# Weight tiles read in runs of two rows (4 KB), two modes on the two halves of the partitions, with the spectrum and the mode products laid out to match

## The chip, the cores and the metric

The kernel runs on one core of one Trainium2 chip. The metric is the device time of one execution in microseconds (us). The kernel before takes 456.14 us, the median of three runs (455.82 to 456.61). The profile is of one execution and spans 453.8 us.

The engines are named as in the profile: PE is TensorE (matmuls; PEld its loads of the stationary operand), DVE is VectorE, ACT is ScalarE, POOL is GpSimd (here it mostly issues transfers), SP is SyncE. SBUF is the memory on the core with 128 partitions, PSUM the memory that the matmuls write.

## The reference

The work has two parts: an attention over 8 batches, 8 heads, 576 positions and 64 values per head, and on its output a spectral mixing with 64 modes, and a residual layer.

```python
# attention, per batch and head
scores = q @ k.T / 8
bias   = -(cum[:, None] - cum[None, :])        # cum = cumsum(max(s, 0))
attn   = softmax(where(causal, -1e9, scores + minimum(bias, 0)))
x      = attn @ v                              # heads side by side: x is [8, 576, 512]

# spectral mixing: w_r, w_i are [64 modes, 512, 512] in float32
X  = rfft(x, axis=1)[:, :64]                   # Xr, Xi
Yr = einsum('bmd,mde->bme', Xr, w_r) - einsum('bmd,mde->bme', Xi, w_i)
Yi = einsum('bmd,mde->bme', Xr, w_i) + einsum('bmd,mde->bme', Xi, w_r)
u  = x + irfft(Yr + 1j * Yi, n=576)
out = u + maximum(u @ w_ch, 0)
```

The two weight tensors hold 2 x 64 x 512 x 512 float32 values, 134.2 MB. Each is used for only eight rows (the batches), so they pass through the core once.

## The kernel before

The 512 channels are taken in NG = 4 groups of 128 (`g`), a group being two heads. There are N = 32 steps of attention (`n`), one for each channel group and batch. The spectrum of a step's output is taken one step later (`fft`), and as soon as a channel group has all its batches, its 64 modes are multiplied with the weights, in NCK = 8 mode groups of MC = 8 modes (`modes(g, c)`). The weights stream in all the while.

A weight tile holds four modes of one channel group: 128 partitions (channels `d`) x 4 modes x 512 (`e`), bf16, 512 KB written and 1 MB of float32 read. There are 128 such tiles, four for each `(g, c)`: real and imaginary (`ri`), even and odd modes (`par`). They go to rings of 11 and 6 buffers, the first eight to places that are free early. GpSimd issues the loads of q, k, v and the weights in one order.

```python
def loads_w(upto):
    ...
        src = (moe_w_r, moe_w_i)[ri]
        todo.append((
            t,                                             # [128, 4, 512] bf16
            src[c * MC + par : (c + 1) * MC : 2, g * P : (g + 1) * P, :].rearrange("m p e -> p m e"),
        ))
        wt[key] = t
    return todo

def load(*lists):                                          # interleaves lists of loads
    todo = [((i + 0.5) / len(l), x) for l in lists for i, x in enumerate(l)]
    for _, (dst, src) in sorted(todo, key=lambda t: t[0]):
        nc.gpsimd.dma_start(out=dst, in_=src)
```

In memory a row of 512 float32 values (2 KB) is contiguous, and the rows of one mode follow each other; a partition takes one row of each of four modes.

The spectrum of one step is a matmul of the step's output (stationary, 128 positions x 128 channels) with a table of sines and cosines (moving, 3 x 64 columns), over five tiles of positions. The result, 128 channels x 192, is cast to bf16 into `xs`, in an order that lets one slice of 32 columns hold 16 values of the spectrum (two of real and imaginary, eight batches) and 16 zeros.

```python
xs = [gp.tile([P, 5, 2, B, NM], BF16, name=f"xs{i}") for i in range(2)]

def fft(n):
    ...
    ps = auxpool.tile([P, 3 * NM], FP32, name="ft_ps", tag="aux")
    for T in range(NT):                                    # NT = 5
        nT = tails[T]
        nc.tensor.matmul(ps, x_all[:nT, g, b, T, :], Ff_sb[:nT, T, :],
                         start=(T == 0), stop=(T == NT - 1))
    for ri in range(2):
        nc.vector.tensor_copy(
            out=xs[g % 2][:, 3 - 2 * ri, :, b, :],
            in_=ps[:, (1 - ri) * NM : (3 - ri) * NM].rearrange("p (r m) -> p r m", r=2),
        )
```

The mode products of one `(g, c)` are 16 matmuls: for each of the four weight tiles (`x`) four modes, each in its own column group (`cg`, 32 output rows) of the array. The zeros in the stationary operand let an even and an odd mode share the 32 output rows of a column group: the even mode adds to 16 of them, the odd mode to the other 16.

```python
def modes(g, c, meanwhile=None):
    ps = auxpool.tile([P, DM], FP32, name="yp", tag="aux")
    for x in range(4):
        ri, par = divmod(x, 2)
        cols = xs[g % 2].rearrange("p k r b m -> p (k r b) m")
        c0 = (48, 16)[ri] - 16 * par
        if meanwhile and x in meanwhile:
            meanwhile[x]()
        for cg in range(4):
            nc.tensor.matmul(
                ps[32 * cg : 32 * cg + 32, :],
                cols[:, c0 : c0 + 32, c * MC + 2 * cg + par],
                wt[(g, c, ri, par)][:, cg, :],
                start=(x == 0), stop=(x == 3),
                tile_position=(0, 32 * cg), skip_group_check=True,
            )
    ...                                                    # sum over g in y_acc (VectorE)
```

After the last step only the mode groups of the last channel group remain (c = 0 to 7), mixed with other products, and then the end: inverse transform, the product with `w_ch`, and the stores. `meanwhile` is used for the very last mode group alone (c = 7): work that needs no weights is put between its tiles.

Of the kernel before, what the change touches and what calls it, by code (L numbers as in the profile page):

```python
# [9 lines left out]
FP32 = mybir.dt.float32  # L10
FP16 = mybir.dt.float16
BF16 = mybir.dt.bfloat16
# [6 lines left out]
def kernel(  # L19
# [26 lines left out]
    MC = 8  # L46
# [7 lines left out]
    W = 2 * P  # L54
    NWN = S // W
    NK = 2 * NWN


    ident_np = np.eye(P, dtype=np.float32)
# [7 lines left out]
    m_idx = np.arange(NM, dtype=np.float64)  # L67
    ang = 2.0 * np.pi * np.outer(t_idx, m_idx) / S
    Ff_np = np.zeros((SP, 3 * NM), dtype=np.float16)
    Ff_np[:S, :NM] = np.sin(ang)  # L70
    Ff_np[:S, NM : 2 * NM] = np.cos(ang)
    Ff_np[:S, 2 * NM :] = -np.sin(ang)
    cmv = np.where(m_idx == 0, 1.0, 2.0) / S
    G_np = np.zeros((NM, 2, SP), dtype=np.float64)
    G_np[:, 0, :S] = cmv[:, None] * np.cos(ang.T)
# [16 lines left out]
    gp = ctx.enter_context(tc.tile_pool(name="globals", bufs=1))  # L92


    x_all = gp.tile([P, NG, B, NT, P], FP16, name="x_all")
    y_acc = gp.tile([P, NCK, DM], FP32, name="y_acc")

    xs = [gp.tile([P, 5, 2, B, NM], BF16, name=f"xs{i}") for i in range(2)]
    ident16h = gp.tile([P, P], FP16, name="ident16h")
    Ff_sb = gp.tile([P, NT, 3 * NM], FP16, name="Ff_sb")  # L100
    G_sb = gp.tile([P, SP], FP16, name="G_sb")
# [4 lines left out]
    auxpool = ctx.enter_context(tc.tile_pool(name="aux_psum", bufs=2, space=PSUM))  # L106
# [24 lines left out]
    p_sb = [ap_.tile([P, poff[-1]], FP16, name=f"p_sb{i}") for i in range(NP_)]  # L131
    p4 = [ap_.tile([P, P], FP16, name=f"p4_{i}") for i in range(2)]

    temp = xs[1].rearrange("p k r b m -> p (k r b m)").bitcast(FP32)
    ident32, negm32, s_sb = temp[:, :P], temp[:, P : P + 2 * W + NL], temp[:NPAIR, -S:]
    ident16 = ap_.tile([P, P], BF16, name="ident16")
    negm = ap_.tile([P, 2 * W + NL], BF16, name="negm")
# [49 lines left out]
    wt = {}  # L187
# [8 lines left out]
    def loads_w(upto):  # L196
        todo = []
        while len(wt) < min(upto, len(wq)):
            g, c, ri, par = key = wq[len(wt)]
            i = ring_of(len(wt))  # L200
            if i is None:
                t = early[len(wt)]
            else:
                t = (wpool, wpool2)[i].tile([P, WM, DM], BF16, name="w_sb", tag="w")
            src = (moe_w_r, moe_w_i)[ri]
            todo.append((
                t,
                src[c * MC + par : (c + 1) * MC : 2, g * P : (g + 1) * P, :].rearrange("m p e -> p m e"),
            ))
            wt[key] = t  # L210
        return todo

# [15 lines left out]
    for n in range(N):  # L228
# [3 lines left out]
        while nt < min(w, len(wq)):  # L232
            i = ring_of(nt)
# [37 lines left out]
    with tc.tile_pool(name="cum_psum", bufs=1, space=PSUM) as cpsum:  # L271
# [5 lines left out]
            out=cum, data0=spos, data1=zer, initial=0.0, op0=ALU.add, op1=ALU.add  # L277
# [133 lines left out]
    def fft(n):  # L411
        if n < 0:
            return
        g, b = divmod(n, B)
        ps = auxpool.tile([P, 3 * NM], FP32, name="ft_ps", tag="aux")
        for T in range(NT):
            nT = tails[T]
            nc.tensor.matmul(  # L418
                ps,
                x_all[:nT, g, b, T, :],  # L420
                Ff_sb[:nT, T, :],
                start=(T == 0), stop=(T == NT - 1),
            )
        for ri in range(2):
            nc.vector.tensor_copy(
                out=xs[g % 2][:, 3 - 2 * ri, :, b, :],
                in_=ps[:, (1 - ri) * NM : (3 - ri) * NM].rearrange("p (r m) -> p r m", r=2),
            )

    def modes(g, c, meanwhile=None):  # L430


        ps = auxpool.tile([P, DM], FP32, name="yp", tag="aux")
        for x in range(4):
            ri, par = divmod(x, 2)
            cols = xs[g % 2].rearrange("p k r b m -> p (k r b) m")
            c0 = (48, 16)[ri] - 16 * par
            if meanwhile and x in meanwhile:
                meanwhile[x]()
            for cg in range(4):  # L440
                nc.tensor.matmul(  # L441
                    ps[32 * cg : 32 * cg + 32, :],
                    cols[:, c0 : c0 + 32, c * MC + 2 * cg + par],
                    wt[(g, c, ri, par)][:, cg, :],
                    start=(x == 0), stop=(x == 3),
                    tile_position=(0, 32 * cg), skip_group_check=True,
                )
        if g == 0:
            nc.vector.tensor_copy(out=y_acc[:, c, :], in_=ps)
        elif g < NG - 1:  # L450
            nc.vector.tensor_tensor(out=y_acc[:, c, :], in0=ps, in1=y_acc[:, c, :], op=ALU.add)
        else:
            yb = spool.tile([P, DM], FP16, name="y_sb", tag="y")
            for cols in halves if c == NCK - 1 else [slice(0, DM)]:
                nc.vector.tensor_tensor(
                    out=yb[:, cols], in0=ps[:, cols], in1=y_acc[:, c, cols], op=ALU.add
                )
            if c >= NCK - 2:
                spread(c, 0, yb)
            return yb  # L460
# [59 lines left out]
    with tc.tile_pool(name="sc_psum", bufs=2, space=PSUM) as scpool, \  # L520
            tc.tile_pool(name="tr_psum", bufs=1, space=PSUM) as trpool, \
            tc.tile_pool(name="av_psum", bufs=1, space=PSUM) as avpool:
        cum_rows(0)
        transposes(0, 0)
        transposes(0, 1)
        load(loads_qkv(2))
        pad_p()
        for n in range(N):
            if n in (0, 2):
                nc.vector.memset(xs[n // 2].rearrange("p k r b m -> p (k r b m)").bitcast(FP32), 0.0)  # L530
            tails_due = loads_tails(n // B + 1)[n % B - 3 : n % B - 2] if 2 < n % B < 5 else []
            load(loads_qkv(n + LA) + tails_due, loads_w(on_chip[n]))
            cum_rows(n + 1)
            scores(n, 0)
            av(n - 1, 1)
            transposes(n + 1, 0)
            scores(n, 1)
            i = first_pairs[n - N + len(first_pairs)] if n >= N - len(first_pairs) else None
            if i is not None:
                first_transposed(i, 0)  # L540
            transposes(n + 1, 1)
            fft(n - 1)
            av(n, 0)
            if i is not None:
                first_product(i, 0)
                first_transposed(i, 1)
            for c in mode_steps.get(n, []):
                modes(c // NCK, c % NCK)
            if i is not None:
                first_product(i, 1)  # L550
            if n == N // 2:
                nc.gpsimd.dma_start(out=wch_sb, in_=moe_w_ch.rearrange("(dt p) e -> p dt e", p=P))
        av(N - 1, 1)
        fft(N - 1)
# [10 lines left out]
    zpool = ctx.enter_context(tc.tile_pool(name="z_psum", bufs=2, space=PSUM))  # L565

    NLOC = 4
    old = xs[0].rearrange("p k r b m -> p (k r b m)")
    xt_sb = [
        old[:, i * 2 * DM : (i + 1) * 2 * DM].bitcast(FP16).rearrange("p (x t c) -> p x t c", x=2, c=P)  # L570
        for i in range(2)
# [199 lines left out]
    c = NCK - 2  # L771
# [112 lines left out]
```

The softmax here doesn't subtract the row's maximum and nothing guards it: scores larger than these inputs give would overflow.

## Time and profile before

| | before |
|---|---|
| time, median of 3 | 456.14 us |
| span of the profile | 453.8 us |
| PE busy | 340.4 us (75%), 4233 instructions |
| DVE busy | 241.0 us (53%), 535 instructions |
| ACT busy | 221.9 us (49%), 390 instructions |
| POOL busy | 183.0 us (40%), 269 instructions |
| weight loads by POOL, 512 KB written each | 120 to the rings and 8 to early places; median 11.9 us from issue to landing in the rings |
| spectrum: matmuls 128*128, 192 columns | 160, median 253 ns each (five overlap to 0.69 us) |
| spectrum: casts to `xs`, 128 x 128 | 64, mean 277 ns |
| mode products 128*32, 512 columns | 512, median 379 ns each (four column groups overlap) |

Busy time counts only the instructions of an engine. The DMA row of the profile is of the 16 engines that move data; its GB/s are the bytes written, so that a load that turns float32 into bf16 shows half of what it reads. The chain of waits follows the work that ended last back in time, at each step to what released it: what is on it sets the end, what is not is hidden.

### The profile page before, as it was taken

The numbers are of one execution on the slowest core, as the hardware profiler recorded it, in microseconds if no ns is written. First come the engines' busy times: TensorE is split into PE (matmuls) and PEld (weight loads), VectorE is DVE, ScalarE is ACT, GpSimd is POOL, SyncE is SP. The second block draws the span as 40 slices with busy tenths as digits, with TensorE's granted clock in tenths as the row PEclk, the third lists the DMA queues.
The fourth block names the chain that finished last, engine by engine and source line by source line (L and its number), as shares of the span: only waits on it lengthen the run. The fifth ranks groups of instructions, "written<-read, shape, count | busy, mean of one in ns | idle before, by whom it ended". The sixth has DMA issues, their size and how long they took to land.

```text
span 453.8 us, 10370 instructions
## 1 busy us (share of the span) xinstructions
PE 340.4 (75%) x4233; PEld 218.6 (48%) x4265; DVE 241.0 (53%) x535; ACT 221.9 (49%) x390; POOL 183.0 (40%) x269
## 2 busy tenths in 40 slices
PE   1779887976563979836677857688889678879995
PEld 1456665654342656624445535456554335534332
DVE  7775665753242656723436434446655443562796
ACT  1585877464242656724435444455551323431774
POOL 6655554554344565434364444444433231200000
PEclk9996999998576889968878899889996986999999
DMA  9999999999999999999999999999999999995688
GB/s 176 200 203 203 202 201 204 202 204 204 205 204 202 201 203 202 205 205 204 202 196 203 204 204 203 204 203 202 206 207 208 207 206 206 207 214 109 232 298 317
DMA packets 108511, 93.75 MB, mean 207 GB/s; under 512 B 28384, under 2 KB 103648, under 8 KB 108464
## 3 DMA queue, kind: packets, MB, share of 16 engines
q0 software_dynamic: 98960, 81.81, 113.8%
q1 hardware_dynamic: 9504, 11.29, 7.8%
q8 instruction: 33, 0.54, 0.4%
q14 instruction: 14, 0.11, 0.1%
HBM read 164.56 MB, written 9.44 MB: 383 GB/s over the span
## 4 chain that ended last, share of the span: by engine, by line
DMA 51%; PE 31%; DVE 8%; issue 4%; POOL 2%; ACT 2%; SPq 0%; DVEq 0%; POOLq 0%; ACTq 0%
DMA w_sb<-in_moe_w_i_dram 21%; DMA q<-in_q_dram 15%; DMA w_sb<-in_moe_w_r_dram 11%; PE sc_ps L365 4%; PE av_ps L394 4%; PE z_ps L602 3%; PE yp L441 3%; PE sc_ps L359 3%; PE tr_ps L324 3%; DMA k<-in_k_dram 2%; PE z_ps L693 2%; PE g_ps L652 2%; PE ft_ps L418 2%; PE u_ps L712 2%; PE u_ps L693 1%
## 5 line engine op out<-in xcount | busy, mean ns | idle before, releaser
L373 ACT ACTIVATE p_sb<-sc_ps,cumt_sb 128x576 f16<-128x576 f32 (+1 forms) x256 | 141.7, 635 | 45.6 <-PE sc_ps L365 45.0
L217 POOL DMA_DIRECT2D w_sb<-in_moe_w_i_dram x60 | 45.1, 751 | 85.0 <-PE yp L441 37.6
L217 POOL DMA_DIRECT2D w_sb<-in_moe_w_r_dram x60 | 45.3, 757 | 63.5 <-DMA w_sb<-in_moe_w_r_dram 28.2
L217 POOL DMA_DIRECT2D v<-in_v_dram x72 | 50.8, 708 | 32.0 <-DMA w_sb<-in_moe_w_r_dram 7.4
L324 PE MATMUL tr_ps<-ident,q 64*64 64x64 bf16 x576 | 17.5, 210 | 54.3 <-DMA q<-in_q_dram 54.3
L359 PE MATMUL sc_ps<-negm,ident 128*128 128x256 bf16 x256 | 55.5, 303 | 0.2
L327 DVE COPY qtA<-tr_ps 64x576 bf16<-64x576 bf16 x32 | 23.8, 743 | 49.6 <-PE tr_ps L324 49.5
L441 PE MATMUL yp<-w_sb,xs 128*32 128x512 bf16 x480 | 36.5, 406 | 14.1 <-DMA w_sb<-in_moe_w_i_dram 11.1
L344 ACT ACTIVATE p<-sc_ps,cumt 128x64 f16<-128x64 f32 x32 | 10.0, 313 | 74.3 <-PE sc_ps L340 74.3
L394 PE MATMUL av_ps<-v,p_sb 128*128 128x65 f16 x1024 | 44.5, 198 | 0.0
L394 PEld LDWEIGHTS <-p_sb 128*128 128x128 f16 x1024 | 39.5, 100 | 4.9 <-issue 0.8
L327 DVE COPY ktA<-tr_ps 64x576 bf16<-64x576 bf16 x32 | 24.0, 749 | 33.6 <-PE tr_ps L324 33.6
L324 PEld LDWEIGHTS <-q 64*64 64x64 bf16 x576 | 13.7, 123 | 57.0 <-DMA q<-in_q_dram 56.3
L365 PE MATMUL sc_ps<-qtB,ktB 128*128 128x64 bf16 (+2 forms) x160 | 34.9, 324 | 3.5 <-issue 2.4
L365 PE MATMUL sc_ps<-qtA,ktA 65*128 65x512 bf16 (+2 forms) x192 | 36.5, 299 | 0.7 <-DMA qtA<-ncum_sb 0.7
L399 DVE TENSOR_REDUCE den<-av_ps 128x5 f32<-128x10 f32 x64 | 10.8, 169 | 49.1 <-PE av_ps L394 48.9
L441 PEld LDWEIGHTS <-xs 128*32 128x32 bf16 x512 | 22.6, 170 | 23.8 <-issue 19.8
L404 DVE TENSOR_TENSOR x_all<-av_ps,rcp 128x320 f16<-128x320 f32 x64 | 31.5, 491 | 2.2
L327 ACT COPY ktB<-tr_ps 64x576 bf16<-64x576 bf16 x32 | 20.3, 634 | 20.3 <-DVE ktA L327 19.4
L365 PEld LDWEIGHTS <-ktB 128*128 128x128 bf16 x192 | 22.4, 117 | 14.8 <-issue 6.3
L324 PE MATMUL tr_ps<-ident,k 64*64 64x64 bf16 x576 | 17.3, 209 | 15.3 <-DVE qtB L327 10.7
L602 PE MATMUL z_ps<-wch_sb,xs 128*128 128x512 f16 x96 | 26.1, 421 | 0.2 <-DVE xs L596 0.2
(117 smaller groups left out, 534.8 us busy)
## 6 DMA issues: line engine op xcount, KB each, us to landing
w_sb<-in_moe_w_r_dram POOLq DMA_DIRECT2D x60, 512.0 KB, 11.9
w_sb<-in_moe_w_i_dram POOLq DMA_DIRECT2D x60, 512.0 KB, 11.9
q<-in_q_dram POOLq DMA_DIRECT2D x32, 144.0 KB, 9.9
k<-in_k_dram POOLq DMA_DIRECT2D x32, 144.0 KB, 10.0
v<-in_v_dram POOLq DMA_DIRECT2D x72, 64.0 KB, 9.7
out_dram<-r_sb SPq DMA_DIRECT2D x16, 256.0 KB, 2.2
out_dram<-r_w SPq DMA_DIRECT2D x16, 256.0 KB, 2.6
x_all<-in_moe_w_i_dram POOLq DMA_DIRECT2D x3, 512.0 KB, 9.9
```

Source lines behind the costliest of these rows:

```text
L217: nc.gpsimd.dma_start(out=dst, in_=src)
L324: nc.tensor.transpose(ps[rows, r, :], src[rows, r, :], ident16[rows, rows])
L327: copy(out=dst[n % NQ][rows, :].rearrange("d (p r) -> d p r", r=R), in_=ps[rows].rearrange("d r p -> d p r"),)
L359: nc.tensor.matmul(ps[:, bass.ds(w * S, W)], ident16, negm[:, bass.ts(r, W)], start=True, stop=False, skip_group_check=True,)
L365: nc.tensor.matmul(ps[:, c0 : c0 + i1 - i0], keys[:, w, r, :], qt[:, i0:i1], start=False, stop=True, skip_group_check=True,)
L373: nc.scalar.activation(out=pt[:, poff[x] : poff[x] + S - w * W], in_=ps[:, w * S : (w + 1) * S - w * W], func=ACTF.Exp, bias=cumt_sb[:, x, ...
L394: nc.tensor.matmul(ps[:, I, r : r + NCH], lhsT, rhs, start=(i == 0), stop=(i == len(todo) - 1), skip_group_check=True,)
L399: nc.vector.tensor_reduce(out=den, in_=ps[:, :, 0 : VW : NCH], axis=mybir.AxisListType.X, op=ALU.add)
L404: nc.vector.tensor_tensor(out=x_all[:, g, b, :, D * h : D * h + D], in0=ps[:, :, 1 : NCH], in1=rcp.unsqueeze(2).to_broadcast([P, NT, D]), ...
L441: nc.tensor.matmul(ps[32 * cg : 32 * cg + 32, :], cols[:, c0 : c0 + 32, c * MC + 2 * cg + par], wt[(g, c, ri, par)][:, cg, :], start=(x == ...
L602: nc.tensor.matmul(z[:, x, :], xts[i][:, x, dt, :], wch_sb[:, dt, :], start=(dt == 0), stop=(last and dt == DT - 1), skip_group_check=True,)
L693: nc.tensor.matmul(dst[x][r, :], G_sb[rows, bass.ds(T * P, r.stop - r.start)], yv[rows, bb, which, :], start=start, stop=True, skip_group_ ...
```

## The change

A partition now takes runs of two consecutive rows of one mode (4 KB read, 2 KB written), so that the number of runs is halved. As a channel group has 128 rows, one mode fills 64 partitions: the tile's four modes stand two by two, one mode on partitions 0 to 63 and the next on 64 to 127. A tile is therefore loaded by two transfers, one for each half. The tile's size and the number of tiles are as before.

The products must find the same channels on the same partitions. Partition `p` of a half holds channels 2p (`q` = 0) and 2p + 1 (`q` = 1), so the spectrum is computed from every second channel, once for each `q`, and for each half only at that half's modes (`h`: even, odd). That makes 20 matmuls of 64 columns of the array where there were five of 128, and four casts on 64 partitions where there were two on 128. `xs` has zeros where a half of the partitions has the other half's mode. A product then sums over 128 partitions: 64 channels of one mode in the upper and 64 of the next mode in the lower half. Their number and shape stay as before; a column group's 32 output rows are, as before, shared by two modes.

The order of the products within a mode group changes: in the common case the two tiles of `ri` are used together, `q` by `q`, with four column groups in turn; in the last mode group they follow the tiles, with two column groups for each.

```diff
@@ -54,6 +54,8 @@
     W = 2 * P
     NWN = S // W
     NK = 2 * NWN
+    HM = NM // 2
+    HP = P // 2
 
 
     ident_np = np.eye(P, dtype=np.float32)
@@ -67,9 +69,9 @@
     m_idx = np.arange(NM, dtype=np.float64)
     ang = 2.0 * np.pi * np.outer(t_idx, m_idx) / S
     Ff_np = np.zeros((SP, 3 * NM), dtype=np.float16)
-    Ff_np[:S, :NM] = np.sin(ang)
-    Ff_np[:S, NM : 2 * NM] = np.cos(ang)
-    Ff_np[:S, 2 * NM :] = -np.sin(ang)
+    for h in range(2):
+        for i, f in enumerate((np.sin(ang), np.cos(ang), -np.sin(ang))):
+            Ff_np[:S, (3 * h + i) * HM : (3 * h + i + 1) * HM] = f[:, h::2]
     cmv = np.where(m_idx == 0, 1.0, 2.0) / S
     G_np = np.zeros((NM, 2, SP), dtype=np.float64)
     G_np[:, 0, :S] = cmv[:, None] * np.cos(ang.T)
@@ -95,7 +97,8 @@
     x_all = gp.tile([P, NG, B, NT, P], FP16, name="x_all")
     y_acc = gp.tile([P, NCK, DM], FP32, name="y_acc")
 
-    xs = [gp.tile([P, 5, 2, B, NM], BF16, name=f"xs{i}") for i in range(2)]
+    xs = [gp.tile([P, 2, 2, 2, 2, B, HM], BF16, name=f"xs{i}") for i in range(2)]
+    xs_flat = [t.rearrange("p q k h r b m -> p (q k h r b m)") for t in xs]
     ident16h = gp.tile([P, P], FP16, name="ident16h")
     Ff_sb = gp.tile([P, NT, 3 * NM], FP16, name="Ff_sb")
     G_sb = gp.tile([P, SP], FP16, name="G_sb")
@@ -131,7 +134,7 @@
     p_sb = [ap_.tile([P, poff[-1]], FP16, name=f"p_sb{i}") for i in range(NP_)]
     p4 = [ap_.tile([P, P], FP16, name=f"p4_{i}") for i in range(2)]
 
-    temp = xs[1].rearrange("p k r b m -> p (k r b m)").bitcast(FP32)
+    temp = xs_flat[1].bitcast(FP32)
     ident32, negm32, s_sb = temp[:, :P], temp[:, P : P + 2 * W + NL], temp[:NPAIR, -S:]
     ident16 = ap_.tile([P, P], BF16, name="ident16")
     negm = ap_.tile([P, 2 * W + NL], BF16, name="negm")
@@ -203,10 +206,14 @@
             else:
                 t = (wpool, wpool2)[i].tile([P, WM, DM], BF16, name="w_sb", tag="w")
             src = (moe_w_r, moe_w_i)[ri]
-            todo.append((
-                t,
-                src[c * MC + par : (c + 1) * MC : 2, g * P : (g + 1) * P, :].rearrange("m p e -> p m e"),
-            ))
+            m0 = c * MC + par * MC // 2
+            for h in range(2):
+                todo.append((
+                    t[HP * h : HP * h + HP].rearrange("p (m q) e -> p m (q e)", q=2),
+                    src[m0 + h : m0 + MC // 2 : 2, g * P : (g + 1) * P, :].rearrange(
+                        "m (p q) e -> p m (q e)", q=2
+                    ),
+                ))
             wt[key] = t
         return todo
 
@@ -412,39 +419,50 @@
         if n < 0:
             return
         g, b = divmod(n, B)
-        ps = auxpool.tile([P, 3 * NM], FP32, name="ft_ps", tag="aux")
-        for T in range(NT):
-            nT = tails[T]
+        ps = auxpool.tile([P, 2, 3 * HM], FP32, name="ft_ps", tag="aux")
+        for q_ in range(2):
+            for T in range(NT):
+                nT = tails[T]
+                for h in range(2):
+                    nc.tensor.matmul(
+                        ps[HP * h : HP * h + HP, q_, :],
+                        x_all[:nT, g, b, T, q_::2],
+                        Ff_sb[:nT, T, 3 * HM * h : 3 * HM * (h + 1)],
+                        start=(T == 0), stop=(T == NT - 1),
+                        tile_position=(0, HP * h), skip_group_check=True,
+                    )
+        for h in range(2):
+            rows = slice(HP * h, HP * h + HP)
+            for k in range(2):
+                nc.vector.tensor_copy(
+                    out=xs[g % 2][rows, :, k, h, :, b, :],
+                    in_=ps[rows, :, k * HM : (k + 2) * HM].rearrange("p q (r m) -> p q r m", r=2),
+                )
+
+    def modes(g, c, meanwhile=None):
+
+
+        ps = auxpool.tile([P, DM], FP32, name="yp", tag="aux")
+        cols = xs[g % 2].rearrange("p q k h r b m -> p q k (h r b) m")
+
+        def product(ri, q_, cg):
             nc.tensor.matmul(
-                ps,
-                x_all[:nT, g, b, T, :],
-                Ff_sb[:nT, T, :],
-                start=(T == 0), stop=(T == NT - 1),
-            )
-        for ri in range(2):
-            nc.vector.tensor_copy(
-                out=xs[g % 2][:, 3 - 2 * ri, :, b, :],
-                in_=ps[:, (1 - ri) * NM : (3 - ri) * NM].rearrange("p (r m) -> p r m", r=2),
-            )
-
-    def modes(g, c, meanwhile=None):
-
-
-        ps = auxpool.tile([P, DM], FP32, name="yp", tag="aux")
+                ps[32 * cg : 32 * cg + 32, :],
+                cols[:, q_, 1 - ri, :, c * MC // 2 + cg],
+                wt[(g, c, ri, cg // 2)][:, 2 * (cg % 2) + q_, :],
+                start=(ri == 0 and q_ == 0), stop=(ri == 1 and q_ == 1),
+                tile_position=(0, 32 * cg), skip_group_check=True,
+            )
+
         for x in range(4):
-            ri, par = divmod(x, 2)
-            cols = xs[g % 2].rearrange("p k r b m -> p (k r b) m")
-            c0 = (48, 16)[ri] - 16 * par
+            ri, y = divmod(x, 2)
             if meanwhile and x in meanwhile:
                 meanwhile[x]()
-            for cg in range(4):
-                nc.tensor.matmul(
-                    ps[32 * cg : 32 * cg + 32, :],
-                    cols[:, c0 : c0 + 32, c * MC + 2 * cg + par],
-                    wt[(g, c, ri, par)][:, cg, :],
-                    start=(x == 0), stop=(x == 3),
-                    tile_position=(0, 32 * cg), skip_group_check=True,
-                )
+            for z in range(4):
+                if meanwhile:
+                    product(ri, z // 2, 2 * y + z % 2)
+                else:
+                    product(ri, y, z)
         if g == 0:
             nc.vector.tensor_copy(out=y_acc[:, c, :], in_=ps)
         elif g < NG - 1:
@@ -527,7 +545,7 @@
         pad_p()
         for n in range(N):
             if n in (0, 2):
-                nc.vector.memset(xs[n // 2].rearrange("p k r b m -> p (k r b m)").bitcast(FP32), 0.0)
+                nc.vector.memset(xs_flat[n // 2].bitcast(FP32), 0.0)
             tails_due = loads_tails(n // B + 1)[n % B - 3 : n % B - 2] if 2 < n % B < 5 else []
             load(loads_qkv(n + LA) + tails_due, loads_w(on_chip[n]))
             cum_rows(n + 1)
@@ -565,7 +583,7 @@
     zpool = ctx.enter_context(tc.tile_pool(name="z_psum", bufs=2, space=PSUM))
 
     NLOC = 4
-    old = xs[0].rearrange("p k r b m -> p (k r b m)")
+    old = xs_flat[0]
     xt_sb = [
         old[:, i * 2 * DM : (i + 1) * 2 * DM].bitcast(FP16).rearrange("p (x t c) -> p x t c", x=2, c=P)
         for i in range(2)
```

More of the change, by code (lines that the diff above doesn't have):

```diff
@@ L434, in modes @@
+        def product(ri, q_, cg):
+            nc.tensor.matmul(
+                ps[32 * cg : 32 * cg + 32, :],
[4 more added lines that the diff above has]
+            )
         for x in range(4):
-            ri, par = divmod(x, 2)
-            cols = xs[g % 2].rearrange("p k r b m -> p (k r b) m")
@@ L437, in modes @@
-            c0 = (48, 16)[ri] - 16 * par
+            ri, y = divmod(x, 2)
             if meanwhile and x in meanwhile:
                 meanwhile[x]()
-            for cg in range(4):
-                nc.tensor.matmul(
-                    ps[32 * cg : 32 * cg + 32, :],
-                    cols[:, c0 : c0 + 32, c * MC + 2 * cg + par],
-                    wt[(g, c, ri, par)][:, cg, :],
-                    start=(x == 0), stop=(x == 3),
-                    tile_position=(0, 32 * cg), skip_group_check=True,
-                )
+            for z in range(4):
[3 more added lines that the diff above has]
+                    product(ri, y, z)
```

## The prediction

> **What bounds the kernel now.** I read the page first: is any engine or the memory path full, and for how long? The slices show it.
>
> ```profile
> PE   1779887976563979836677857688889678879995
> DMA  9999999999999999999999999999999999995688
> GB/s 176 200 203 203 202 201 204 202 204 204 205 204 202 201 203 202 205 205 204 202 196 203 204 204 203 204 203 202 206 207 208 207 206 206 207 214 109 232 298 317
> DMA packets 108511, 93.75 MB, mean 207 GB/s; under 512 B 28384, under 2 KB 103648, under 8 KB 108464
> ...
> q0 software_dynamic: 98960, 81.81, 113.8%
> ...
> HBM read 164.56 MB, written 9.44 MB: 383 GB/s over the span
> ```
>
> See that DMA stays full for 36 of 40 slices, about 410 us, at a nearly constant 200 to 207 GB/s, while PE has free tenths everywhere. The GB/s are counted on the written side: weights are read as float32 and written as bf16, so 206 GB/s written is 412 read. Of 164.56 MB read, 134.2 MB are weights (2 x 64 x 512 x 512 x 4 B). The q0 count can be rebuilt: 128 weight tiles x 512 rows, 512 rows of w_ch, 64 q and k loads x 128, 64 v loads x 256, 8 tail loads x 512, and 16 completion packets for each of 265 transfers, in all 98,960. One packet is one contiguous run.
>
> Then the chain of waits, for where the DMA stops setting the end:
>
> ```profile
> 328.07 14.09 DMA w_sb<-in_moe_w_i_dram
> ...
> 353.00 19.81 DMA w_sb<-in_moe_w_i_dram
> 372.80 0.04 issue
> 372.85 0.59 PE yp L441 x4
> ...
> 415.38 0.43 PE yp L441 x4
> 415.82 0.44 DVE y_sb L455
> ```
>
> The last transfer on the chain lands at 372.8 us. It is weight tile 112 of 128, the last one of mode group c = 3 of the fourth channel group. After it there is only compute, 81 us of it. Yet the last 16 tiles are still arriving; at 2.54 us each the last lands near 372.8 + 40.6 = 413.4, and PE uses it at 415.3. So the transfers after 372.8 are hidden, but with only about 2 us to spare.
>
> Third, windows by stage, for how much PE could be slowed before it matters:
>
> ```profile
> core 0: us, PE busy (x), PEclk, DMA share, GB/s
> 12.00:96.00 84.00, 72.53 (x1142) 0.96 1.31 202
> 96.00:342.00 246.00, 174.55 (x2441) 0.85 1.29 203
> 342.00:373.00 31.00, 24.25 (x184) 0.83 1.24 207
> 373.00:416.00 43.00, 35.75 (x294) 0.88 1.16 197
> ```
>
> PE has 11.5 us free in the first 84, 71 us in the next 246, 6.8 us in the next 31. After 373 its gaps are waits on DVE and ACT, none on DMA.
>
> Last, the packet records that the trace keeps. In 100 to 330 us a packet starts on its DMA engine 12.8 ns after one with a 256 B source run, 22.2 after 512 B, 78.8 after 2048 B (weights) and 88.2 after 2304 B (q, k). A straight line fits all four: 3.35 ns per packet plus 0.03685 ns per byte read. After a completion packet (4 B) the next starts 21 ns later. So a weight tile costs each of the 16 engines 32 x 78.8 + 21 = 2,543 ns, which is the spacing at which the queue drains late in the kernel (issues 345.29 to 380.98, 14 intervals: 2.549 us).
>
> **What the Trainium skill says.** "DMA: Bandwidth & Descriptors", section "Why small descriptors are slow (HBM only)", gives trn2 a fixed overhead of about 3 cycles per packet beside 32 B per cycle. The trace agrees: 3.35 ns is 2.8 cycles of 32 B at the fitted 27.1 GB/s. The same page, "Why a DMA increments its semaphore by 16 and not by 1", says that a GpSimd transfer posts a completion from all 16 engines; the count above agrees (16 x 265). Its "Rules for kernel authors" advise against splitting a transfer over partition halves, since both halves use the same engines. "SBUF — State Buffer", section "Door 1: The DMA port swizzle (why `[64,N]` ≈ `[32,N]`)", says that partitions 0..63 reach 8 of the 16 write ports, and 64..127 the other 8, with an asymptote near 218 GB/s for such a half. No transfer in this trace shows that limit: weights go to all 128 partitions, and the only loads on 64 partitions are the eight small tails.
>
> **The change part by part.**
>
> *Packets.* A tile's rows become 4 KB runs: 16 packets per engine instead of 32. By the line, 4096 B take 3.35 + 150.9 = 154.3 ns. Each tile is now two transfers, so two completions: 16 x 154.3 + 2 x 21 = 2,511 ns, against 2,543. That is 32 ns saved per tile, 1.3%: halving the packets gives 53 ns, the second completion takes 21 back. Only the 112 tiles before the gate at 372.8 count: 112 x 32 ns = 3.6 us.
>
> *GpSimd.* 128 more transfers to issue. A q load (128 runs) takes 550 ns of GpSimd, a v load (256 runs) 703, a weight tile (512 runs) 750; a half tile has 128 runs in two levels, so I take 0.6 us. Two make 1.2 us per tile for 2.5 us of transfer. In steady state a step issues 10 halves and four q, k, v loads: 6 + 2.5 = 8.5 us of GpSimd in 15 us. No bound. The timeline shows eight transfers in flight at most (the tile issued at 353.00 lands 19.81 us later, 7.8 intervals of 2.54). Eight halves are still 10 us of work in the queue. Nothing from this.
>
> *Spectrum.* Per head pair 20 matmuls of 64 columns x 96 instead of 5 of 128 x 192. Today five take 0.69 us. Of the narrow kind, eight 128*64 matmuls of 128 columns last 0.57 us at best, 71 ns each, so 20 are about 1.3 us: +0.65 us per pair, x 32 = 21 us of PE. VectorE gets two more casts of 272 ns per pair: +17 us in all. Both lie where PE has room: 8 pairs x 0.65 = 5 us of 11.5 free in 12:96, 15 of 71 in 96:342. On the path: 0, or a fraction of a microsecond early on.
>
> *Mode products.* Still 16 matmuls of 128*32 with 512 columns per mode group; the zero blocks of the stationary operand move with the layout. Two small losses. In group c = 3 the last tile now gates six matmuls instead of four: +0.2 us. In the last group the order by tile means that only two of the four column groups work together. Sixteen over four groups take 1.12 us today, 0.28 per four; over two groups four should take about 0.48. Four times 0.2 us: +0.8 us, in the stretch that PE sets.
>
> *Clearing.* Two clears of 5120 bf16 become 4096, 2.19 to 1.75 us each, on VectorE; not on the path after the start.
>
> Sum: -3.6 + 0.2 + 0.8 = -2.6 us, 453.5 us, if the write side takes it.
>
> **The rivals.**
>
> *Write ports.* A half tile goes to one set of eight ports. If the engines stay in step, two share one port. Each writes 2048 B per 154.3 ns, 13.3 GB/s; two are 26.5, against the 27.2 per port that the skill's page implies. That is 97% of the port with no overhead of its own. If the port also loses some 3 cycles per packet, the pair takes 134 cycles for a run against 131 on the read side: the packet is back at about 157 ns and the saving gone, leaving the second completion. That makes +2.4 us (112 x 21 ns) +1.0: 459.5. If sharing costs 5% of the weights' time, 112 x 2.54 x 5% = 14 us: 468. For it: the page measures 64 partitions as poor as 32, and the order of the halves is the same on all engines, so they tend to stay together. Against: the reads set the pace, the written bytes are half of them, and q, k, v loads spread the engines again.
>
> *The transfers are hidden anyway.* The chain has DMA at 51% of the span, and after 372.8 nothing. For it: PE is 78% busy in 342:373. Against: in 300:417 PE still waits 6.6 us for weights, more than the 3.6 I credit. A gain above 6 us would meet this wall, so it caps the best case near 449.
>
> *PE becomes the bound in the first 90 us.* Windows 36:48 shows PE 11.95 of 12 us busy at clock 0.75. If the spectrum costs twice my estimate, 8 x 1.3 = 10 us fills the room there; since GpSimd issues in order behind buffers that PE frees, 1 to 3 us of it could come through: 455 to 457. In the profile DMA was full there, so I give it little.
>
> **Range and chances.** Packet arithmetic alone gives 453.5. I put about half on that outcome, a quarter on the saving being eaten (457 to 460), a quarter on a real loss at the ports or by issue (460 to 470). The middle is 455.0. The range 449.0 to 466.0 goes from the cap to a port loss of 4%. Faster by over 2% means below 447.0, 9.1 us; the packet overhead altogether is worth less, so 0.05. Slower by over 2%, above 465.3, needs the ports to bind: 0.19. Within 2%: 0.76.
>
> **What would show it.** q0 must have 68,240 packets (32,768 of 4 KB for the weights, 29,184 others, 16 x 393). Right: GB/s in 342:373 near 209 instead of 207, the last chained transfer landing near 369, spectrum matmuls 1.3 us per pair with no new wait on them, the last mode group 0.8 us longer. Ports: GB/s at or below 207 where weights flow alone, with a higher DMA share per byte. GpSimd: waits before weight loads ending in "issue", DMA tenths below 9 before 370. I am wrong if PE waits for spectrum casts, or if the gain exceeds 6 us.

## The result, and the profile after

| | before | after |
|---|---|---|
| time, median | 455.98 us (4 runs, one more than above) | 453.74 us (4 runs, 452.44 to 454.76) |
| ratio, 95% interval | | 0.9946 (0.9924 to 0.9968) |
| span of the profiled run | 453.8 us | 452.6 us |
| PE busy | 340.4 us, 4233 instructions | 355.4 us, 4745 instructions |
| DVE busy | 241.0 us | 257.5 us |
| POOL busy | 183.0 us, 269 instructions | 241.2 us, 397 instructions |

The change makes the kernel half a percent faster. First the lines of the page after that answer to those of before: the load of PE and of the DMA engines in 40 slices, and the queues.

```profile
PE   1789998997674989956787868789888859879995
DMA  9999999999999999999999999999999999993688
GB/s 179 202 203 205 204 203 205 202 207 206 208 207 202 200 190 202 208 207 206 204 194 207 207 207 205 207 205 203 210 209 211 209 209 209 210 217 75 234 297 316
DMA packets 77796, 93.83 MB, mean 207 GB/s; under 512 B 30432, under 2 KB 40160, under 8 KB 77744
...
q0 software_dynamic: 68240, 81.81, 104.6%
...
HBM read 164.56 MB, written 9.44 MB: 384 GB/s over the span
```

The bytes are the same; the packets of q0 fell from 98,960 to 68,240, the number worked out in advance. Where weights flow almost alone the rate rose by some 3 GB/s (slices 29 to 35, counted from 1: 210, 209, 211, 209, 209, 209, 210 after, 206 to 208 before). But in slices 14 and 15 it now falls to 200 and 190, where before it was 201 and 203; slice 21 is slow in both (194 after, 196 before).

The windows by stage, PE alone (columns: stretch, its length, PE busy and instructions, granted clock, DMA share, GB/s written):

```profile
core 0: us, PE busy (x), PEclk, DMA share, GB/s
12.00:96.00 84.00, 73.50 (x1249) 0.98 1.23 204
96.00:342.00 246.00, 189.61 (x2845) 0.85 1.19 205
342.00:373.00 31.00, 23.49 (x188) 0.83 1.12 210
```

PE took on 15 us of work between 96 and 342 us and 1 us before; both stretches had room for it. And the chain of waits, at the two places that matter:

```profile
360.08 10.08 DMA w_sb<-in_moe_w_i_dram
370.20 1.09 PE yp L449 x5
...
414.01 0.60 PE yp L449 x4
414.63 0.44 DVE y_sb L473
```

The tile that gates the end (number 112, group c = 3) lands at 370.16 us instead of 372.80. From there to the end of the span it is 82.4 us, before 81.0. So in these two profiles 2.6 us came at the gate and 1.4 were given back behind it; the second profile of the changed kernel, below, shows how much of the 1.4 is the change.

What a packet costs is read from the packet records of the two traces: the time from one packet's start to the next on the same DMA engine, for packets of one size in a row.

```
source run   before      after      line 3.35 ns + 0.03685 ns per byte
  256 B      12.8 ns     12.9 ns
  512 B      22.2 ns     22.2 ns
 2048 B      78.8 ns     -          weights before
 2304 B      88.2 ns     88.2 ns
 4096 B      -           154 ns     weights after: the line gives 154.3
completion   21 ns       21 ns
```

The 4 KB packet lies on the line that was drawn through the others. With 128 more transfers, 16 completions each, the queue's ledger to the gate is: weights 112 x (32 x 78.8 - 16 x 154.2) ns = -6.1 us, completions 112 x 21 ns = +2.4 us. That makes -3.7 us, and -2.6 were seen. The missing 1.1 us fits time in which the engines had too little to do. An estimate from the slices: slices 13 to 16 fall short of the 207 around them by 34 in sum, 34 / 207 x 11.3 us = 1.9 us, where before they fell short of 205 by 12, 0.7 us.

### The profile page after: what moved, and what is told of

It is laid out like the page before. It is cut to its first block, busy times and chain, and to the rows that moved or that the text cites. A ratio compares the mean times of both kernels' runs of the same rounds, so it can differ in the third digit from the quotient of the medians.

```text
span 452.6 us, 11579 instructions
## 1 busy us (share of the span) xinstructions
PE 355.4 (79%) x4745; PEld 224.4 (50%) x4745; DVE 257.5 (57%) x599; ACT 221.9 (49%) x390; POOL 241.2 (53%) x397
## 3 DMA queue, kind: packets, MB, share of 16 engines
q0 software_dynamic: 68240, 81.81, 104.6%
## 4 chain that ended last, share of the span: by engine, by line
DMA 58%; PE 27%; DVE 5%; issue 4%; POOL 4%; ACT 1%; DVEq 0%; POOLq 0%; ACTq 0%
DMA w_sb<-in_moe_w_i_dram 29%; DMA k<-in_k_dram 9%; DMA q<-in_q_dram 8%; DMA w_sb<-in_moe_w_r_dram 7%; PE yp L449 3%; PE av_ps L401 3%; PE sc_ps L372 2%; PE ft_ps L427 2%; PE z_ps L620 2%; PE tr_ps L331 2%; PE z_ps L711 2%; DMA x_all<-in_moe_w_r_dram 2%; PE sc_ps L366 2%; PE g_ps L670 2%; DMA y_acc<-in_moe_w_r_dram 2%
## 5 line engine op out<-in xcount | busy, mean ns | idle before, releaser
L224 POOL DMA_DIRECT2D w_sb<-in_moe_w_r_dram x120 | 71.5, 596 | 63.1 <-DMA w_sb<-in_moe_w_r_dram 20.6
L224 POOL DMA_DIRECT2D w_sb<-in_moe_w_i_dram x120 | 71.5, 597 | 49.8 <-DMA w_sb<-in_moe_w_i_dram 18.8
L366 PE MATMUL sc_ps<-negm,ident 128*128 128x256 bf16 x256 | 54.4, 297 | 0.2
L449 PE MATMUL yp<-w_sb,xs 128*32 128x512 bf16 x480 | 37.8, 423 | 11.2 <-DMA w_sb<-in_moe_w_i_dram 6.8
L372 PE MATMUL sc_ps<-qtB,ktB 128*128 128x512 bf16 (+2 forms) x192 | 42.1, 335 | 0.0
L437 DVE CAST xs<-ft_ps 64x128 bf16<-64x128 f32 x128 | 31.4, 284 | 10.0 <-PE ft_ps L427 9.6
L427 PE MATMUL ft_ps<-Ff_sb,x_all 128*64 128x96 f16 (+1 forms) x640 | 34.8, 232 | 1.0 <-DVE x_all L411 1.0
L449 PEld LDWEIGHTS <-xs 128*32 128x32 bf16 x512 | 19.2, 146 | 23.2 <-issue 9.7
```

What stands on the lines that cost most here:

```text
L366: nc.tensor.matmul(ps[:, bass.ds(w * S, W)], ident16, negm[:, bass.ts(r, W)], start=True, stop=False, skip_group_check=True,)
L372: nc.tensor.matmul(ps[:, c0 : c0 + i1 - i0], keys[:, w, r, :], qt[:, i0:i1], start=False, stop=True, skip_group_check=True,)
L427: nc.tensor.matmul(ps[HP * h : HP * h + HP, q_, :], x_all[:nT, g, b, T, q_::2], Ff_sb[:nT, T, 3 * HM * h : 3 * HM * (h + 1)], start=(T == ...
L437: nc.vector.tensor_copy(out=xs[g % 2][rows, :, k, h, :, b, :], in_=ps[rows, :, k * HM : (k + 2) * HM].rearrange("p q (r m) -> p q r m", r=2),)
L449: nc.tensor.matmul(ps[32 * cg : 32 * cg + 32, :], cols[:, q_, 1 - ri, :, c * MC // 2 + cg], wt[(g, c, ri, cg // 2)][:, 2 * (cg % 2) + q_, ...
```

## The experiments

My theory was: a packet costs 3.35 ns beside its bytes and a completion 21 ns on each engine; the weights' stream up to tile 112 sets the end; everything else that the change adds is hidden, but for the order of the products in the last stage. The rivals: shared write ports on a half of the partitions; the new layout, not the loads, brings or costs time; the short transfers leave the queue dry. All ratios are to the kernel before on the same chip.

### The split alone

```diff
-            todo.append((t, src[c * MC + par : (c + 1) * MC : 2, g * P : (g + 1) * P, :].rearrange(...)))
+            for h in range(2):      # kernel before; RP = 64
+                todo.append((
+                    t[RP * h : RP * h + RP],
+                    src[c * MC + par : (c + 1) * MC : 2, g * P + RP * h : g * P + RP * h + RP, :].rearrange(...),
+                ))
```

> The kernel before, with each weight tile loaded by two transfers on the two halves of the partitions, and runs of 2 KB as they were. Packet theory (a packet costs 3.35 ns plus 0.03685 ns per byte read, a completion 21 ns on each engine): 32 x 78.8 + 2 x 21 = 2,564 ns per tile instead of 2,543, so the tile that gates the end lands 112 x 21 ns = 2.4 us later. Time 458.3 us, ratio to before about 1.005. Port theory (two engines on one write port of a half): the packets of the weights start more than 78.8 ns apart, and the loss is larger, 1.01 or more. If only the length of the queue (eight transfers in flight, now of half the size) counts: dry spots of the DMA in single slices, up to 1 us on top, 1.007.

Measured: 459.15 us, ratio 1.0064 (1.0049 to 1.0078). The packets of the weights start 78.8 ns apart as before, so the ports cost nothing. The gate lands at 377.05 us, 4.2 later, of which the second completion explains 2.4. The rest shows in the slices of the page:

```profile
GB/s 179 198 201 202 201 199 201 202 203 203 203 203 198 188 202 201 203 204 203 200 183 201 202 203 203 201 201 199 200 205 206 205 205 205 205 212 122 227 294 317
```

Slices 14 and 21 fall to 188 and 183 GB/s: about (15 + 20) / 203 x 11.4 us = 2 us of the engines' time. The kernel before held part of this already: 201 and 196 there, (3 + 8) / 204 x 11.3 us = 0.6 us. In the profiled run the delay grows large enough that the last tile, hidden before, sets the end (the chain's last transfer):

```profile
408.66 10.76 DMA w_sb<-in_moe_w_i_dram
419.42 0.04 issue
419.46 0.47 PE yp L444 x4
```

### The same number of transfers without halves

```diff
+            for h in range(2):      # kernel before: two modes per transfer, all partitions
+                m0 = c * MC + par + 4 * h
+                todo.append((
+                    t[:, 2 * h : 2 * h + 2, :],
+                    src[m0 : m0 + 3 : 2, g * P : (g + 1) * P, :].rearrange("m p e -> p m e"),
+                ))
```

> The kernel before, with each weight tile loaded by two transfers of two modes each, both on all 128 partitions, runs of 2 KB. As many transfers and completions as in the split over the halves of the partitions, but no transfer is confined to half of them. That split cost a ratio of 1.0064, of which the second completion explains 1.005; the rest was seen as lost time of the DMA engines near 157 us and 237 us. If that rest comes from the number of transfers (eight in flight, now of half the size): again 1.006 to 1.007 and slices below 195 GB/s at the same two places. If it comes from the halves of the partitions: 1.005 and no such slices.

Measured: 458.49 us, ratio 1.0053 (1.0040 to 1.0066). The intervals of the two splits overlap, so their times don't decide between the two explanations. The slices (page):

```profile
GB/s 175 198 201 202 201 200 202 202 203 203 204 203 198 194 201 200 204 204 203 201 195 202 202 203 203 203 202 199 201 205 207 205 205 205 205 213 125 228 297 317
```

Slice 14 dips again, about half as deep (194; 188 with the halves, 201 before), so the number of transfers alone can bring a dip there. Slice 21 (195) stands where it stood in the kernel before (196): the deeper dip of the other split (183) came with the halves or by chance. One profile of each split doesn't decide, so whether the halves cost anything stays open. The size fits the second completion: 2.4 us expected, 2.4 us measured (458.49 against 456.11). In the profile the gate lands at 375.76 us, 3.0 later than before.

### The new layout with the old loads

```diff
-            for h in range(2):
-                todo.append((t[HP * h : HP * h + HP]..., src[m0 + h : m0 + MC // 2 : 2, ...]...))
+            todo.append((
+                t, src[m0 : m0 + MC // 2, g * P : (g + 1) * P, :].rearrange("m p e -> p m e"),
+            ))
```

> The changed kernel with one transfer of 2 KB runs per tile, as before the change; the spectrum and the products stay in the new layout, so that channels meet the wrong partitions (the sums are over the wrong rows, their number and shape are unchanged). Packet theory: the whole gain of the change goes, and its small costs at the two ends of the last stage stay: 0.3 us in the last mode group, 0.5 us in the group behind the gate. Ratio to before 1.002, time 456.8 us. Rival, the spectrum's extra matmuls and casts cost time as well: 1.005 or more, and the tile behind the gate lands later than 373 us. Rival, the gain came from the new layout and not from the loads: 0.995 as in the changed kernel.

Measured: 457.16 us, ratio 1.0023 (1.0014 to 1.0033). So the spectrum's 480 more matmuls and 64 more casts, with all other parts of the layout, cost about 1 us; the gain of the change comes from the loads. The page shows no dip at slice 15 (202, 202 and 200 GB/s in slices 14 to 16). Its gate landed at 373.98 us, a microsecond later than in the profile before: of the cost, more may lie ahead of the gate than I expected, but one profile each doesn't settle a microsecond.

### One transfer of 4 KB runs

```diff
+            m1, r0 = m0 + 2 * (g % 2), 2 * P * (g // 2)      # changed kernel; two modes, 256 rows
+            todo.append((
+                t.rearrange("p (m q) e -> p m (q e)", q=2),
+                src[m1 : m1 + 2, r0 : r0 + 2 * P, :].rearrange("m (p q) e -> p m (q e)", q=2),
+            ))
```

> The changed kernel with one transfer per tile, all 128 partitions, in runs of 4 KB: a tile takes 256 rows of two modes, so that every weight is still read once, but the rows meet the wrong channels and modes (same bytes, same products). Packet theory: 16 x 154.2 + 21 = 2,488 ns per tile instead of 2,509; the gate 2.4 us earlier than in the changed kernel, and 0.8 us more if its dry spot near 166 us came from the short queue: about 450.7 us, ratio to before 0.988. If completions cost nothing in a full queue: as the changed kernel, 0.995. If halves had shared write ports: packets now nearer together than 154 ns.

Measured: 450.87 us, ratio 0.9882 (0.9866 to 0.9898), 0.2 us from the estimate. The page and the chain of waits of this kernel:

```profile
GB/s 174 202 205 207 205 205 207 206 208 208 209 208 204 204 195 204 209 209 208 205 205 208 208 208 207 208 207 206 212 210 212 211 211 211 211 218 68 236 301 316
DMA packets 75747, 93.81 MB, mean 209 GB/s; under 512 B 28384, under 2 KB 38112, under 8 KB 75696
```

```profile
350.33 17.40 DMA w_sb<-in_moe_w_i_dram
367.73 0.04 issue
367.77 1.08 PE yp L447 x6
```

The gate lands 2.4 us before that of the changed kernel, as the completions alone would have it. This kernel drops the second completion and the halves together; the tiles of eight modes, below, drop the completion and keep the halves, and take the same time. The packets still start 154 ns apart: on all partitions or on half, the same. The dip at slice 21 has gone (205), but the one at slice 15 stays (195). By the sum used above, slices 13 to 16 fall short of 208 by 25 here, 25 / 208 x 11.2 us = 1.3 us, against 1.9 in the changed kernel and 0.7 before. So the short queue can explain about half of the dip at most: a kernel with a queue of full-sized transfers has the rest too, once the weights arrive faster.

### Tiles of eight modes

Here the second completion is saved with every row in its own place. Each transfer carries four modes to a half of the partitions.

```diff
-    WA, WB = 11, 6
+    WA, WB = 6, 3                      # changed kernel; tiles of eight modes
-    wq = [(g, c, ri, par) ...]         # 128 tiles
+    wq = [(g, c, ri) ...]              # 64 tiles; three early places
-                    src[m0 + h : m0 + MC // 2 : 2, ...]
+                    src[m0 + h : m0 + MC : 2, ...]
-                wt[(g, c, ri, cg // 2)][:, 2 * (cg % 2) + q_, :],
+                wt[(g, c, ri)][:, 2 * cg + q_, :],
-                if meanwhile:
-                    product(ri, z // 2, 2 * y + z % 2)
-                else:
-                    product(ri, y, z)
+                product(ri, y, z)
-    yb = modes(NG - 1, NCK - 1, {2: first_u, 3: first_z})
+    yb = modes(NG - 1, NCK - 1, {2: lambda: (first_u(), first_z())})
```

Small buffers of the end take halves of a tile; the schedule of the loads counts in eights (two tiles at the start, then two and three in turn).

> The changed kernel with tiles of eight modes instead of four, still two transfers per tile on the two halves, so one completion per megabyte as before the change, rings of 6 and 3 such tiles, and four column groups in turn in every mode group. Packet theory: per eight modes 32 x 154.2 + 2 x 21 = 4,976 ns instead of 5,019; the gate 2.4 us earlier than in the changed kernel, the dry spot of 0.8 us gone, the last mode group 0.3 us shorter: about 450.2 us, ratio to before 0.987. Rival, coarser buffers: PE waits for a whole tile of eight modes, or a load waits for a whole buffer, and DMA tenths fall below 9 before 370 us: 0.995 or worse.

Measured: 450.84 us, ratio 0.9890 (0.9868 to 0.9913): 1.1% faster than before, and its interval lies below that of the changed kernel's second measurement (0.9931 to 0.9961). The page and the chain:

```profile
GB/s 174 203 204 205 202 195 203 200 209 208 208 209 206 203 184 205 207 208 208 209 201 208 208 207 208 209 206 206 210 211 213 210 211 210 212 218 78 235 300 316
```

```profile
349.44 19.89 DMA w_sb<-in_moe_w_i_dram
369.32 0.04 issue
369.37 0.68 PE yp L449 x8
```

The rate between the dips is that of the single transfer (208 to 213). But there are dips at slices 6, 8 and 15 (195, 200, 184), and in this profile the gate came only 0.8 us before that of the changed kernel, not 2.4. The profiled run, at 452.4 us, is 1.6 us above the median, so its gate may be late for this kernel. Whether the order of issue or the coarser buffers made the dips is what the next kernel asks.

### The same with earlier loads

```diff
-        w = W0 + (WA + WB + NE - W0) * (n + 1) // (B + 1) if n < B else on_chip[-1] + 2 + n % 2
+        w = W0 + (WA + WB + NE - W0) * (n + 1) // B if n < B else on_chip[-1] + 3
```

> The kernel with tiles of eight modes, with the loads of weights moved earlier in the order of issue (all twelve buffers due by the eighth step instead of ten, and up to three tiles per step instead of two and a half; the free buffers still set the limit). The tiles of eight modes lost 1.6 us of the engines' time, between 54 and 81 us and near 160 us. If that was the order of issue: 0.986 to 0.987 (449.5 us) and no slice below 200 GB/s before 90 us. If the buffers set it: 0.989 as it was, with the same slices; if q, k and v now come later than PE needs them: 0.99 or more.

Measured: 451.76 us, ratio 0.9898 (0.9879 to 0.9917), no different from the one before. The dips before 90 us went (203, 205, 207 GB/s in slices 6 to 8), so these were the order of issue; but a dip of 188 came at slice 21. By the medians nothing was won. The profile alone would say otherwise: its gate lands at 367.71 us, 1.6 earlier than in the profile before it, but it is of the fastest of six runs (449.84 us), and that one of a run above its median.

### The changed kernel again

> The changed kernel itself once more, with more rounds, beside the other kernels of this call: 0.9946 as before, with a narrower interval; from the ledger of the packets (weights -6.2 us, completions +2.4, lost time of the engines +1.0, other +0.3, end of the last stage +0.8) -1.7 us or 0.9963 would be the lower end, and 0.992 without the lost time.

Measured: 453.67 us, ratio 0.9946 (0.9931 to 0.9961), 2.4 us less than before, where the ledger gave 1.7 at its lower end. The slices of this profile are 196 and 193 GB/s at 14 and 15 (200 and 190 in the first profile) and 200 at 21 (194 in the first): the dip near 166 us is in both, the one at slice 21 changes by 6 GB/s between two runs of the same kernel. This run is also needed to read what happens behind the gate. First the last mode group before, then in this run of the changed kernel (timeline of PE):

```profile
411.04 0.69 PE L441 MATMUL yp<-w_sb,xs 128*32 128x512 bf16 x8
...
413.06 0.47 PE L441 MATMUL yp<-w_sb,xs 128*32 128x512 bf16 x4
...
415.30 0.47 PE L441 MATMUL yp<-w_sb,xs 128*32 128x512 bf16 x4
```

```profile
407.90 0.67 PE L449 MATMUL yp<-w_sb,xs 128*32 128x512 bf16 x8
...
409.90 0.65 PE L449 MATMUL yp<-w_sb,xs 128*32 128x512 bf16 x4
...
412.34 0.65 PE L449 MATMUL yp<-w_sb,xs 128*32 128x512 bf16 x4
```

Four products that share two column groups take 0.65 us instead of 0.47, twice. The first eight stand together and still use all four groups: 0.67 against 0.69. So the order of the last group costs 0.35 us (from its start to the last sum 5.13 us against 4.78). In this run the six matmuls behind the gate take 0.65 us (before, the four behind the gate took 0.57, in part at half the clock; four took 0.48 at 370.32 us, where the granted clock was 1.00), in the first profile of the change 1.07. From gate to end it is 80.6 us in this run and 82.4 in the other, for the same kernel: about a microsecond of the 1.4 that the first profile "gave back" is not the change.

The three profiles differ in the first 17 us behind the gate, up to the start of the same product (z_ps from xs), and the clock granted to PE there differs with them. Before, the first profile of the change, and this run (columns: stretch, length, PE busy with its instructions, granted clock, DMA share, GB/s):

```profile
372.80:389.00 16.20, 12.74 (x97) 0.68 1.24 206
```

```profile
370.20:387.50 17.30, 13.89 (x99) 0.65 1.12 209
```

```profile
370.40:385.80 15.40, 11.92 (x98) 0.78 1.12 209
```

The six products behind the gate show it most plainly: 1.07 us where the granted clock was 0.50 (370.0 to 371.3 us, first profile), 0.65 us where it was 1.00 (the same stretch of this run). From the z_ps product to the end the three profiles take 64.8, 65.1 and 65.2 us. So what the change itself costs behind the gate is 0.65 - 0.48 = 0.17 us for the two more products and 0.35 us in the last group; with 2.4 to 2.6 us won at the gate that leaves some 2 us, and the medians say 2.2 and 2.4.

## Why the prediction was right, point by point

- **Packets.** Right. 154.3 ns predicted, 154 measured; 2,511 ns per tile predicted, 16 x 154.2 + 42 = 2,509 measured. The single transfer, the split by modes and the tiles of eight modes confirm the 2.4 us of the second completion to within half a microsecond; the split over halves lost 0.8 us more (459.15 against 455.96).
- **The gate.** Right in place, too large in size: -3.6 us predicted, -2.6 in the first profile and -2.4 in the second. The term "nothing from this" for the queue of shorter transfers was the one that failed: about 1.1 us of engine time is lost, most of it near 166 us. The split by modes shows that more transfers alone make a dip near there; the single transfer shows that a faster stream makes one too.
- **Spectrum.** Right that it is hidden in the main. The matmuls are cheaper than I took them: 20 take 0.91 us at their fastest, not 1.3 (and my own 20 x 71 ns come to 1.4). The casts are a little dearer, 284 ns on 64 partitions, not 272. With the old loads the whole layout costs 1.2 us, of which 0.5 are the two losses named next; where the rest falls is not shown. Of the 15 us by which PE is busier, the spectrum explains 32 x (0.91 - 0.69) = 7 us at their fastest; the split alone, with the instructions of the kernel before, already shows 349.8 us busy against 340.4. From the chain of waits of the changed kernel:

```profile
48.40 0.91 PE ft_ps L427 x20
```

- **Mode products.** The sign was right, the size not: the last group loses 0.35 us instead of 0.8, because I counted four slow sets of products where only two stand alone, while the products behind the gate lose 0.17 us, near the 0.2, once runs of the same clock are compared.
- **PE as the bound in the first 90 us.** Not so: between 12 and 96 us PE was busy for 73.5 of 84 us, and the stream ran at 204 GB/s instead of 202.
- **GpSimd.** Right in its cost: 0.60 us per half tile assumed, 0.597 measured. That the queue was never short was wrong, as said under the gate.

The groups of weight loads and casts after, on which the points on GpSimd and the spectrum rest (columns: busy us and mean ns, then idle time before and its releaser):

```profile
L224 POOL DMA_DIRECT2D w_sb<-in_moe_w_r_dram x120 | 71.5, 596 | 63.1 <-DMA w_sb<-in_moe_w_r_dram 20.6
L224 POOL DMA_DIRECT2D w_sb<-in_moe_w_i_dram x120 | 71.5, 597 | 49.8 <-DMA w_sb<-in_moe_w_i_dram 18.8
...
L437 DVE CAST xs<-ft_ps 64x128 bf16<-64x128 f32 x128 | 31.4, 284 | 10.0 <-PE ft_ps L427 9.6
```

- **The sum.** The arithmetic alone gave 453.5 us, and 453.74 came: in part by luck, since two of its errors cancel by half: the gate gave 1.0 to 1.2 us less than predicted, and the work behind it lost about 0.5 less. I had moved the number to 455.0 for the rival of the write ports. That rival is gone: packets of half a tile start as close together as those of a full one. The Trainium skill's "SBUF — State Buffer", section "Door 1: The DMA port swizzle (why `[64,N]` ≈ `[32,N]`)", made it plausible; here the engines wrote 210 GB/s to one half after the other, under the 218 that the section gives for a half, so its limit was not reached and is not refuted.
- **Transfers hidden anyway.** Not so: the gain at the gate came through to the end.
- **The halves.** The advice in the Trainium skill's "DMA: Bandwidth & Descriptors", section "Rules for kernel authors", against splitting over partition halves, agrees with the runs: each split costs 21 ns per engine and tile, and the tiles of eight modes, which keep the halves but save that completion, were faster than the changed kernel. What the change bought with the split, the longer runs, was worth more.

Still open is why the engines run short near 166 us. In the changed kernel GpSimd stood still before a weight load for 1.95 us for which the profile names nothing, and a few microseconds later the rate was down. The timeline of GpSimd, and then the windows of 3 us:

```profile
160.91 0.57 POOL L224 DMA_DIRECT2D q<-in_q_dram  x1
163.43 0.60 POOL L224 DMA_DIRECT2D w_sb<-in_moe_w_r_dram  x1 [1.95 <-issue]
```

```profile
162.00:165.00 3.00, 2.04 (x29) 1.36 (x30) 1.72 (x3) 0.68 (x3) 1.57 (x3) 0.83 1.32 191
165.00:168.00 3.00, 3.00 (x56) 2.09 (x55) 1.09 (x3) 2.58 (x5) 3.00 (x6) 0.60 1.05 175
168.00:171.00 3.00, 2.64 (x43) 1.66 (x40) 2.44 (x8) 0.00 (x0) 1.64 (x3) 1.00 1.16 201
```

(Columns: stretch, length, then PE, PEld, DVE, ACT and POOL busy with their instructions, granted clock, DMA share, GB/s.) The eight transfers issued before 163.43 are three of v, two of q, one of k and two half tiles, so there was little left in flight. GpSimd pauses at the same place in the other kernels that dip there: 2.04 us in the second profile of the changed kernel, 2.92 in the tiles of eight modes with earlier loads, and in the kernel with one transfer and in the tiles of eight modes:

```profile
163.62 0.70 POOL L222 DMA_DIRECT2D w_sb<-in_moe_w_i_dram  x1 [3.13 <-PE tr_ps L329]
```

```profile
165.04 0.62 POOL L224 DMA_DIRECT2D w_sb<-in_moe_w_i_dram  x1 [3.03 <-PE av_ps L401]
```

The kernels without a dip there wait a little less before a weight load in 150 to 170 us: 1.83 us at most with the old loads under the new layout, and 1.69 at most before the change:

```profile
161.01 0.74 POOL L217 DMA_DIRECT2D w_sb<-in_moe_w_r_dram  x1 [1.69 <-PE sc_ps L365]
```

So a likely account is that GpSimd, issuing in order, waits there for work of PE while the faster stream empties the queue. It is not shown: no run took this wait or the small transfers away, and the two splits dip a little earlier without any pause above 1.5 us.

## What to carry to other kernels

Where the DMA engines are full, take their time apart into packets and completions before touching anything: a straight line through the packet sizes that a trace already holds predicted the time of a size that was not in it. Longer runs that cost more transfers give part of their gain back; here the second completion took back 2.4 of 6.1 us, and larger tiles, not only longer runs, made the faster kernel. Then ask what the faster stream meets: a gain of a per cent in the transfers was trimmed by dips of a microsecond at places that the slices of the page show at once.

## What was not expected of the hardware

GpSimd's time to issue a transfer follows the partitions more than the runs: 64 partitions with two runs each took 597 ns, with four runs 618 to 624, but 128 partitions with two runs 704 and with four runs 751. And the cost of a completion, 21 ns, is more than a quarter of that of a 2 KB packet, though it carries 4 bytes.
